# Attention with beacon keys followed by a two-layer MoE block: head pairs scored in two PSUM banks, values as the moving operand, 512-token chunks, and other loads for Q and K

## The chip, the cores and the metric

The kernel runs on one core of a Trainium2 chip. Five engines work side by side on their own instruction queues: TensorE (PE in the profile, its weight loads as PEld), VectorE (DVE), ScalarE (ACT), GpSimd (POOL) and SyncE (SP). Data comes from device memory by DMA transfers, which here are issued from the queues of POOL and SP. Matrix products go into PSUM, which has eight banks of 512 four-byte columns per partition. What counts is the device time of one execution in microseconds, as the median of several runs.

## What is computed

The inputs are fp32: q, k, v of 8 batches, 8 heads, 576 positions and 64 features; 16 beacon keys and values per head that every query sees; and two weight matrices.

```python
k_all = concatenate([beacon_k, k], axis=2)          # 592 keys
v_all = concatenate([beacon_v, v], axis=2)
scores = matmul(q, k_all.T) / 8
scores = where(causal, -1e9, scores)                # beacons are never masked
a = exp(scores - scores.max(-1)); a /= a.sum(-1) + 1e-9
x = matmul(a, v_all)                                # (8, 8, 576, 64)
x = x.transpose(0, 2, 1, 3).reshape(4608, 512)      # tokens x (heads, features)
h = x @ w_in                                        # 512 -> 2048
out = maximum(0.01 * h, h) @ w_out                  # 2048 -> 512
```

## The kernel before

A scheduler of the framework puts the instructions of each engine in an order that follows the written program with some reordering by readiness. Each engine then runs its own queue strictly in that order, and waits on semaphores where it needs another engine's result or a free buffer.

**Loads.** For each batch q, k and v are fetched by POOL's DMA queue in blocks of 128 positions, which also turns fp32 into bf16 on the way (`load_q`, `load_k`, `load_v`, L121 to L160); the beacons are the first 16 rows of the key blocks. The value tile `v_aug` holds 64 value columns and 64 columns of ones per head. The weights come in 16 loads from the same queue, spread over the first twelve steps.

**Heads.** The program runs 64 steps, one head each. In every second step `stage_transpose` (L162) turns two heads of q and k so that features lie on partitions: two heads fill 128 partitions, and DVE copies them out of PSUM. `stage_scores` (L185) takes one head, 64 partitions: for each block of 128 keys one matmul gives transposed scores (keys on partitions, queries along columns), only for the queries that see the block, and ACT takes the exponential of each block into `aT` (L202), six instructions a head. DVE zeroes the masked triangles by a multiplication (L209, L217). There is no maximum subtraction.

**Values.** `stage_av` (L225) makes the value block the stationary operand and `aT` the moving one, in two halves of 288 queries. The result has the 64 value features on partitions 0 to 63 and, from the ones, 64 copies of the row sum on partitions 64 to 127. The reciprocal is taken on ACT as exp(-ln(sum)):

```python
nc.scalar.activation(out=lnd[0:64, 0:qw], in_=av[64:128, 0:qw], func=AF.Ln)
nc.scalar.activation(out=recip[0:64, 0:qw], in_=lnd[0:64, 0:qw], func=AF.Exp, scale=-1.0)
```

and DVE multiplies by it on the way into `xT` (L249), which already has features on partitions, as the MoE part needs it.

**MoE.** For each batch of 576 tokens `moe1_fchunk` (L256) computes one of 16 blocks of 128 hidden features, in a piece of 512 tokens and one of 64, and ACT applies the leaky ReLU as Prelu (L271). `moe2_tchunk` (L278) accumulates 16 matmuls for 128 tokens and DVE copies the result out (L290); the 64 left-over tokens of two batches share one tile (`moe2_tailpair`, L293). The tables `MOE1_SCHED`, `MOE2A_SCHED` and `MOE2B_SCHED` place this work beside the heads of the next batches, and the last batch's part follows alone.

**PSUM.** Two banks' worth for transposes, four for scores and MoE together (`ps_acc`), two for the values.

Of the kernel before, what the change touches and what calls it, by code (L numbers as in the profile page):

```python
# [15 lines left out]
def kernel(  # L16
# [15 lines left out]
    L = S + NB  # L32
# [3 lines left out]
    assert DM == H * D  # L36

    KBLK = []
    l0 = 0
    while l0 < L:  # L40
        rows = min(128, L - l0)
        off = max(0, l0 - NB)
        KBLK.append((l0, rows, off, S - off))
        l0 += 128
    NKB = len(KBLK)

    QBLK = []
    s0 = 0
    while s0 < S:
        rows = min(128, S - s0)  # L50
        QBLK.append((s0, rows))
        s0 += 128
    NQB = len(QBLK)

    NJ = DM // 128
    NF = DF // 128
    TOKCH = [(0, 512), (512, S - 512)]
    OTCH = [(i * 128, min(128, S - i * 128)) for i in range((S + 127) // 128)]

    QCH = [(0, 288), (288, 288)]  # L60

    singles = ctx.enter_context(tc.tile_pool(name="singles", bufs=1))
    inpool = ctx.enter_context(tc.tile_pool(name="inpool", bufs=2))
    headpool = ctx.enter_context(tc.tile_pool(name="headpool", bufs=2))
    xpool = ctx.enter_context(tc.tile_pool(name="xpool", bufs=2))
# [3 lines left out]
    ps_tr = ctx.enter_context(tc.tile_pool(name="ps_tr", bufs=2, space=bass.MemoryType.PSUM))  # L69
    ps_acc = ctx.enter_context(tc.tile_pool(name="ps_acc", bufs=4, space=bass.MemoryType.PSUM))  # L70
    ps_av = ctx.enter_context(tc.tile_pool(name="ps_av", bufs=2, space=bass.MemoryType.PSUM))

    ident = singles.tile([128, 128], BF16, name="ident")
    with tc.high_priority():
        make_identity(nc, ident)

    mask_reg = singles.tile([128, 128], BF16, name="mask_reg")
    with tc.high_priority():
        nc.vector.memset(mask_reg, 1.0)
        nc.gpsimd.affine_select(  # L80
            out=mask_reg,
            in_=mask_reg,
            compare_op=ALU.is_ge,
            fill=0.0,
            base=0,
            channel_multiplier=-1,
            pattern=[[1, 128]],
        )

    w_in_sb = singles.tile([128, NJ, DF], BF16, name="w_in_sb")  # L90
# [5 lines left out]
    def _w_in_load(j, half):  # L96
        f0 = half * (DF // 2)
        return lambda: nc.gpsimd.dma_start(
            out=w_in_sb[:, j, f0 : f0 + DF // 2],
            in_=w_in_r[:, j, f0 : f0 + DF // 2],  # L100
        )

    def _w_out_load(c):
        return lambda: nc.gpsimd.dma_start(
            out=w_out_sb[:, c : c + 2, :], in_=w_out_r[:, c : c + 2, :]
        )

    weight_loads = []
    for half in range(2):
        for j in range(NJ):  # L110
            weight_loads.append(_w_in_load(j, half))
    for c in range(0, NF, 2):
        weight_loads.append(_w_out_load(c))

    def alloc_batch():
        q_nat = inpool.tile([128, NQB, H, D], BF16, name="q_nat")
        k_nat = inpool.tile([128, NKB, H, D], BF16, name="k_nat")
        v_aug = inpool.tile([128, NKB, H, D + 64], BF16, name="v_aug")
        return dict(q_nat=q_nat, k_nat=k_nat, v_aug=v_aug)

    def load_q(b, bt):  # L121
        q_nat = bt["q_nat"]
        for ci, (s0, rows) in enumerate(QBLK):
            nc.gpsimd.dma_start(  # L124
                out=q_nat[0:rows, ci, :, :],
                in_=q[b, :, s0 : s0 + rows, :].rearrange("h p d -> p h d"),
            )

    def load_k(b, bt):
        k_nat = bt["k_nat"]  # L130
        nc.gpsimd.dma_start(
            out=k_nat[0:NB, 0, :, :],
# [309 lines left out]
```

## Time and profile before

| | |
|---|---|
| median of 3 runs | 616.53 us (lowest 613.58) |
| span of the profiled execution, first to last instruction | 610.7 us |
| time of the profiled execution itself | not recorded apart from its span |
| matmul and weight-load instructions on PE | 2766 and 2816 recorded |
| ACT table loads at L243 and L246 | 80 and 79 |
| read from and written to device memory | 37.22 MB, 9.44 MB |

A row of the groups names the source line, the engine, the operation, the tiles written and read, the shapes and a count; behind the bar stand the busy time in us, the mean duration of one in ns, and the time the engine sat idle just ahead of these instructions with what ended it. A row of the timeline has the start and the duration in us, the engine, the line, and a count of merged instructions, with the idle time ahead of it in brackets. A row of the windows has the stretch and its length, the busy time of PE, PEld, DVE, ACT and POOL with counts, the granted clock of PE as a share of full speed, the DMA share and GB/s. Matmuls overlap in the record: the distance from start to start tells their pace, the duration does not.

### The profile page before, as it was taken

How to read it: one execution, taken by the hardware profiler on the slowest of the kernel's cores; microseconds unless marked ns; L12 is line 12 of the kernel's file. 1: busy time of each engine (PE TensorE's matmuls, PEld its weight loads, DVE VectorE, ACT ScalarE, POOL GpSimd, SP SyncE). 2: the span in 40 equal slices, each digit the busy share in tenths (PEclk: the TensorE clock that was granted, in tenths of full speed). 3: DMA queues.
4: the chain of work that ended last, by engine and by line, in shares of the span. 5: the costliest groups of instructions: out<-in, count | busy, mean ns of one | idle time of the engine just before them, and what ended most of it. 6: DMA issues, size and time to landing. Idle time of an engine off the chain costs nothing.

```text
span 610.7 us, 7832 instructions
## 1 busy us (share of the span) xinstructions
PE 470.3 (77%) x2766; PEld 226.2 (37%) x2816; DVE 174.1 (29%) x557; ACT 512.6 (84%) x1057; POOL 120.4 (20%) x159
## 2 busy tenths in 40 slices
PE   2867677876798697886888777886858876885696
PEld 1323333433344343443444333443424433442342
DVE  4233321342124412234223521234122421132101
ACT  0899989998999969999999979999799978997640
POOL 9885323020230303103230302303000000000000
PEclk9999888996889988997989978899789988897799
DMA  9999638024660706606561526616000100000002
GB/s 93 152 176 170 41 25 55 35 48 27 40 41 34 75 18 41 57 35 58 38 42 36 64 29 39 41 53 57 1 1 18 52 4 15 0 35 18 19 18 69
DMA packets 123432, 28.57 MB, mean 47 GB/s; under 512 B 115712, under 2 KB 117760, under 8 KB 123392
## 3 DMA queue, kind: packets, MB, share of 16 engines
q0 software_dynamic: 118144, 18.62, 41.3%
q1 hardware_dynamic: 5248, 9.44, 4.5%
q8 instruction: 22, 0.36, 0.3%
q14 instruction: 18, 0.15, 0.1%
HBM read 37.22 MB, written 9.44 MB: 76 GB/s over the span
## 4 chain that ended last, share of the span: by engine, by line
ACT 51%; PE 24%; issue 16%; DVE 6%; POOL 1%; DMA 1%; DVEq 0%; POOLq 0%
ACT L243 14%; PE acc L260 11%; ACT aT L202 11%; ACT L246 9%; ACT recip L246 6%; ACT lnd L243 6%; PE acc L195 5%; ACT gT L271 4%; PE acc L282 4%; DVE osb L290 3%; DVE xT L249 3%; PE acc L296 2%; PE av_ps L233 1%; ACT gtail L271 1%; DMA k_nat<-in_k_dram 1%
## 5 line engine op out<-in xcount | busy, mean ns | idle before, releaser
L260 PE MATMUL acc<-xT,w_in_sb 128*128 128x512 bf16 (+1 forms) x996 | 169.9, 329 | 33.0 <-ACT gT L271 25.2
L202 ACT ACTIVATE aT<-acc 128x512 bf16<-128x512 f32 (+5 forms) x384 | 123.6, 408 | 38.7 <-PE acc L195 37.5
L233 PE MATMUL av_ps<-aT,v_aug 128*128 128x288 bf16 (+4 forms) x512 | 85.3, 273 | 59.1 <-DVE xT L249 59.1
L260 PEld LDWEIGHTS <-w_in_sb 128*128 128x128 bf16 x1024 | 82.7, 111 | 118.9 <-issue 77.8
L249 DVE TENSOR_TENSOR xT<-av_ps,recip 64x288 bf16<-64x288 f32 x128 | 53.5, 447 | 253.9 <-ACT recip L246 253.8
L282 PE MATMUL acc<-w_out_sb,gT 128*128 128x512 bf16 x491 | 114.4, 382 | 0.8
L195 PE MATMUL acc<-qT_sb,kT_sb 64*128 64x512 bf16 (+5 forms) x384 | 82.6, 310 | 30.1 <-ACT gT L271 13.9
L243 ACT ACT_TABLE_LOAD x80 | 102.6, 1283 | 1.4
L246 ACT ACT_TABLE_LOAD x79 | 101.4, 1283 | 1.4
L271 ACT ACTIVATE gT<-acc 128x512 bf16<-128x512 f32 x128 | 76.6, 599 | 28.9 <-PE acc L260 26.6
L233 PEld LDWEIGHTS <-v_aug 128*128 128x128 bf16 (+1 forms) x512 | 41.0, 101 | 107.4 <-issue 80.6
L282 PEld LDWEIGHTS <-gT 128*128 128x128 bf16 x512 | 48.8, 98 | 54.7 <-issue 1.6
L124 POOL DMA_DIRECT2D q_nat<-in_q_dram x40 | 33.9, 878 | 98.1 <-PE tp_ps L168 95.1
L246 ACT ACTIVATE recip<-lnd 64x288 f32<-64x288 f32 x128 | 51.4, 436 | 0.9
L217 DVE TENSOR_TENSOR aT<-aT,mask_reg 128x128 bf16<-128x128 bf16 (+1 forms) x256 | 45.9, 212 | 18.8 <-ACT aT L202 16.4
L195 PEld LDWEIGHTS <-kT_sb 64*128 64x128 bf16 (+1 forms) x384 | 28.7, 102 | 59.8 <-issue 48.6
L243 ACT ACTIVATE lnd<-av_ps 64x288 f32<-64x288 f32 x128 | 46.9, 403 | 4.2 <-PE av_ps L233 3.3
L209 DVE TENSOR_TENSOR aT<-aT,mask_reg 128x112 bf16<-128x112 bf16 x64 | 13.5, 211 | 81.3 <-ACT aT L202 80.3
L148 POOL DMA_DIRECT2D v_aug<-in_beacon_v_dram x8 | 4.4, 548 | 156.2 <-PE av_ps L233 156.0
L140 POOL DMA_DIRECT2D k_nat<-in_k_dram x40 | 33.6, 861 | 1.4 <-DMA w_in_sb<-in_moe_w_in_dram 0.7
L157 POOL DMA_DIRECT2D v_aug<-in_v_dram x40 | 33.7, 868 | 0.0
L290 DVE COPY osb<-acc 128x512 f32<-128x512 f32 x32 | 21.9, 684 | 33.4 <-PE acc L282 33.0
(23 smaller groups left out, 185.0 us busy)
## 6 DMA issues: line engine op xcount, KB each, us to landing
out_dram<-osb SPq DMA_DIRECT2D x32, 256.0 KB, 2.0
q_nat<-in_q_dram POOLq DMA_DIRECT2D x32, 128.0 KB, 4.1
k_nat<-in_k_dram POOLq DMA_DIRECT2D x24, 128.0 KB, 4.1
v_aug<-in_v_dram POOLq DMA_DIRECT2D x24, 128.0 KB, 4.2
w_in_sb<-in_moe_w_in_dram POOLq DMA_DIRECT2D x8, 256.0 KB, 7.0
w_out_sb<-in_moe_w_out_dram POOLq DMA_DIRECT2D x8, 256.0 KB, 9.0
out_dram<-osb SPq DMA_DIRECT2D x8, 128.0 KB, 2.3
k_nat<-in_k_dram POOLq DMA_DIRECT2D x8, 112.0 KB, 3.2
```

The source lines that it names most:

```text
L124: nc.gpsimd.dma_start(out=q_nat[0:rows, ci, :, :], in_=q[b, :, s0 : s0 + rows, :].rearrange("h p d -> p h d"),)
L195: nc.tensor.matmul(out=acc[0:rows, 0:cw], lhsT=kT_sb[p0 : p0 + 64, l0_ : l0_ + rows], rhs=qT_sb[p0 : p0 + 64, c0 : c0 + cw], start=True, s ...
L202: nc.scalar.activation(out=aT[0:rows, ci, c0 - off : c0 - off + cw], in_=acc[0:rows, 0:cw], func=AF.Exp, scale=0.125,)
L217: nc.vector.tensor_tensor(out=aT[0:rows, ci, 0:rows], in0=aT[0:rows, ci, 0:rows], in1=mask_reg[0:rows, 0:rows], op=ALU.mult,)
L233: nc.tensor.matmul(out=av[0:128, lo - qs : qw], lhsT=v_aug[0:rows, ci, h, :], rhs=aT[0:rows, ci, lo - off : qs + qw - off], start=(bi == 0 ...
L243: nc.scalar.activation(out=lnd[0:64, 0:qw], in_=av[64:128, 0:qw], func=AF.Ln)
L246: nc.scalar.activation(out=recip[0:64, 0:qw], in_=lnd[0:64, 0:qw], func=AF.Exp, scale=-1.0)
L249: nc.vector.tensor_tensor(out=xT[(h % 2) * 64 : (h % 2) * 64 + 64, h // 2, qs : qs + qw], in0=av[0:D, 0:qw], in1=recip[0:64, 0:qw], op=ALU ...
L260: nc.tensor.matmul(out=acc[:, 0:tw], lhsT=w_in_sb[:, j, fc * 128 : (fc + 1) * 128], rhs=xT[:, j, ts : ts + tw], start=(j == 0), stop=(j == ...
L271: nc.scalar.activation(out=dst, in_=acc[:, 0:tw], func=AF.Prelu, alpha=0.01,)
L282: nc.tensor.matmul(out=acc[0:tw, :], lhsT=gT[:, fc, t0 : t0 + tw], rhs=w_out_sb[:, fc, :], start=(fc == 0), stop=(fc == NF - 1),)
L290: nc.vector.tensor_copy(out=osb[0:tw, :], in_=acc[0:tw, :])
```

## The change

Nearly all of the kernel is written anew; the mathematics is the same.

- **Loads of q and k.** They come as fp32 by SP's DMA queue, in pieces of two heads with 96 partitions and six successive positions (1536 bytes) each; POOL casts them to bf16 (for the first batch DVE casts q). Beacon keys are loaded apart, turned once per batch on PE, and copied by POOL into the first 16 columns of each `kT`. Position p x 6 + i lies on partition p, so the copies out of PSUM write with a step of six.
- **Weights** come in eight loads of twice the size, all issued in the first three steps.
- **Scores** are made for two heads at once, one on partitions 0 to 63 and one on 64 to 127, into the two banks of one PSUM tile, and one exponential covers both banks: five exponentials per pair of heads. The last 128 queries of key block 0 are packed beside block 2, and block 4 is padded to 128 queries.
- **Values.** `aT` is now the stationary operand and the value block with a single column of ones the moving one, 65 columns wide; 30 matmuls a pair. The sum lies in column 64 of each query's row; DVE takes the reciprocal and multiplies, and PE turns the result into `xT` by five transposes.
- **MoE** runs over nine chunks of 512 tokens across batch borders, all tiles full, in 40 steps of 16 + 16 matmuls. `xT` holds all tokens.
- **ACT tables.** One load of a set is placed at the start.
- **PSUM.** Four banks for scores (two tiles of two banks), two for transposes and values together (`mb`), two for the MoE.

The core of the new code (line numbers of the new kernel are L195 for `scores`, L246 for `values`, L288 for `moe1`):

```diff
+    nc.scalar.preload_act_table_set("natural_log_exp_and_others")
+    def load_qk(b, half, split):
...
+            raw = rawpool.tile([RP, 4, RI, D], FP32, name=name)
+            for e in range(2):
+                hs = slice(h0 + 2 * e, h0 + 2 * e + 2)
+                nc.sync.dma_start(
+                    out=raw[:, 2 * e : 2 * e + 2],
+                    in_=src[b, hs].rearrange("h (p i) d -> p h i d", i=RI),
+                )
+            for e in range(2):
+                eng = (nc.vector if n == 0 else nc.gpsimd) if split else nc.gpsimd
+                eng.tensor_copy(
+                    out=dst[:, :, h0 + 2 * e : h0 + 2 * e + 2, :],
+                    in_=raw[:, 2 * e : 2 * e + 2].rearrange("p h i d -> p i h d"),
+                )
+    def transposes(g):
...
+        for par in range(2):
+            ps_ = slice(par * 64, par * 64 + 64)
+            nc.gpsimd.tensor_copy(out=kT[ps_, 0:NB], in_=bkT[ps_, b, 2 * hp + par, :])
+        for src, dst in ((q_nat, qT), (k_nat, kT[:, NB : NB + S])):
+            ps = ps_mb.tile([128, 1024], BF16, name="mb", tag="mb")
+            for i in range(RI):
+                nc.tensor.transpose(
+                    ps[:, i * RP : (i + 1) * RP],
+                    src[:, i, hs, :].rearrange("p h d -> p (h d)"),
+                    ident[0:RP, 0:RP],
+                )
+            nc.vector.tensor_copy(
+                out=dst.rearrange("c (p i) -> c i p", i=RI),
+                in_=ps[:, 0:S].rearrange("c (i p) -> c i p", i=RI),
+            )
+    def scores(g):
...
+        for parts in SCORES:
+            sc = ps_sc.tile([128, 2, 512], FP32, name="sc", tag="sc")
+            c0 = parts[0][3]
+            for c, q0, w, col in parts:
+                for par in range(2):
+                    ps_ = slice(par * 64, par * 64 + 64)
+                    nc.tensor.matmul(
+                        out=sc[0 : ROWS[c], par, col - c0 : col - c0 + w],
+                        lhsT=kT[ps_, c * 128 : c * 128 + ROWS[c]],
+                        rhs=qT[ps_, q0 : q0 + w],
...
+            nc.scalar.activation(
+                out=aT[:, :, c0 : c0 + w], in_=sc[:, :, 0:w], func=AF.Exp, scale=0.125
+            )
...
+    def values(g):
...
+                    for c in range(t + 1):
+                        a0 = acol(c, q0)
+                        nc.tensor.matmul(
+                            out=avv[:, n, 0 : D + 1],
+                            lhsT=aT[0 : ROWS[c], par, a0 : a0 + 128],
+                            rhs=va[0 : ROWS[c], c, 2 * hp + par, :],
...
+            nc.vector.reciprocal(out=rec[:, n0:n1], in_=avv[:, :, D])
+            nc.vector.tensor_tensor(
+                out=x_nat[:, t0:t1].rearrange("p t e d -> p (t e) d"),
+                in0=avv[:, :, 0:D],
+                in1=rec[:, n0:n1, None].to_broadcast([128, n1 - n0, D]),
+                op=ALU.mult,
+            )
...
+    for g in range(NG + 2):
...
+            transposes(g)
+        if 1 <= g <= NG:
+            scores(g - 1)
+        if g >= 2:
+            values(g - 2)
+        if g >= NPAIR + 2:
+            moe_step(g - NPAIR - 2)
+    for m in range(NG - NPAIR, NPAIR * (NCH + 1)):
+        moe_step(m)
```

A step g thus makes the transposes of pair g, the scores of pair g - 1, the values of pair g - 2, and from g = 6 on one of the 40 MoE steps.

Three places show how the change moves instructions. ACT first, before: what follows the scores of one head (lnd and recip are the logarithm and the reciprocal of the row sums, aT the exponentials).

```order
L243 ACT_TABLE_LOAD
L243 ACTIVATE lnd<-av_ps 64x288 x2
L246 ACT_TABLE_LOAD
L246 ACTIVATE recip<-lnd 64x288 x2
L202 ACTIVATE aT<-acc 128x512
L202 ACTIVATE aT<-acc 128x64
L202 ACTIVATE aT<-acc 128x464
L202 ACTIVATE aT<-acc 128x336
L202 ACTIVATE aT<-acc 128x208
L202 ACTIVATE aT<-acc 80x80
```

ACT after, from its first instruction on (sc is the PSUM tile of two banks):

```order
L77 ACT_TABLE_LOAD
L215 ACTIVATE aT<-sc 128x2x512
L215 ACTIVATE aT<-sc 128x2x464 x2
L215 ACTIVATE aT<-sc 128x2x208
L219 ACTIVATE aT<-sc 80x2x128
```

Ten instructions a head, two of them loads, have become five for two heads; behind each pair's five stand four Prelus from the seventh pair on, and no further load.

POOL near the start, before: its queue behind the first k loads.

```order
L148 DMA v_aug<-in_beacon_v_dram 16x8x64
L157 DMA v_aug<-in_v_dram 112x8x64
L157 DMA v_aug<-in_v_dram 128x8x64 x3
L157 DMA v_aug<-in_v_dram 80x8x64
L98 DMA w_in_sb<-in_moe_w_in_dram 128x1024 x3
L124 DMA q_nat<-in_q_dram 128x8x64 x4
```

POOL after, at the same place (k_raw and q_raw are the fp32 tiles, the L178 copies write the beacon columns of kT):

```order
L160 DMA v_aug_95<-in_v_dram 128x8x64 x3
L164 DMA v_aug_95<-in_v_dram 80x8x64
L108 DMA w_in_sb<-in_moe_w_in_dram 128x4x512 x2
L137 CAST q_nat<-q_raw 96x6x128 x2
L137 CAST k_nat<-k_raw 96x6x128 x2
L108 DMA w_in_sb<-in_moe_w_in_dram 128x4x512 x2
L178 COPY kT<-bkT 64x16 x2
L146 DMA bk<-in_beacon_k_dram 128x64 x2
```

Before, POOL only issued transfers here; now casts of the next batch and the copies that the scores of pair 0 wait for stand in the same queue, behind value and weight loads.

PE in the middle of the program, before: between two groups of score matmuls (L195) stand value matmuls with 176 and 48 moving columns.

```order
L195 MATMUL acc<-qT_sb,kT_sb 128x64
L233 LDWEIGHTS v_aug
L233 MATMUL av_ps<-aT,v_aug 128x176
L233 LDWEIGHTS v_aug
L233 MATMUL av_ps<-aT,v_aug 128x48
```

PE after, in the middle, from the second block of scores (L204) to the values (L261):

```order
L204 MATMUL sc<-qT,kT 128x464
L293 LDWEIGHTS w_in_sb
L293 MATMUL acc<-xT,w_in_sb 128x512
L261 LDWEIGHTS aT
L261 MATMUL mb<-v_aug_96,aT 128x65
```

The values are loaded as weights no more: `aT` is, and each load is followed by 65 moving columns; a MoE matmul stands between the scores and the values.

More of the change, by code (lines that the diff above doesn't have):

```diff
@@ L31 @@
     NB = beacon_k.shape[2]
-    L = S + NB
     DM = moe_w_in.shape[0]
@@ L112 @@
[L112 to L123, printed above, removed]
+    xT = singles.tile([128, NJ, NTOK], BF16, name="xT")
```

459 lines of the change are left out of this document (178 added, 281 removed).

## The prediction

> **What bounds the kernel now.** I read the page's busy shares first, then its clock row, the chain of work that ended last, the groups kept apart by shape, and the timeline at four places.
>
> ```profile
> span 610.7 us, 7832 instructions
> PE 470.3 (77%) x2766; PEld 226.2 (37%) x2816; DVE 174.1 (29%) x557; ACT 512.6 (84%) x1057; POOL 120.4 (20%) x159
> ACT 51%; PE 24%; issue 16%; DVE 6%; POOL 1%; DMA 1%; DVEq 0%; POOLq 0%
> L243 ACT ACT_TABLE_LOAD x80 | 102.6, 1283 | 1.4
> L246 ACT ACT_TABLE_LOAD x79 | 101.4, 1283 | 1.4
> L249 DVE TENSOR_TENSOR xT<-av_ps,recip 64x288 bf16<-64x288 f32 x128 | 53.5, 447 | 253.9 <-ACT recip L246 253.8
> ```
>
> ACT is busy 84% of the span and holds half of the chain. Of its 512.6 us, 102.6 + 101.4 = 204 us are table loads: each head switches to the logarithm and back. The last row shows who suffers: DVE, and behind it PE, wait 253.8 us for that reciprocal. PE's 77% is not a full PE, as matmuls overlap in the record, so its true pace must come from distances between starts:
>
> ```profile
> 572.68 15.70 PE L260 MATMUL acc<-xT,w_in_sb 128*128 128x512 bf16 x110 [0.15 <-ACT gT L271]
> 588.22 13.98 PE L282 MATMUL acc<-w_out_sb,gT 128*128 128x512 bf16 x63
> 602.03 3.62 PE L296 MATMUL acc<-w_out_sb,gtail 128*128 128x512 bf16 x15
> 580.47 0.60 ACT L271 ACTIVATE gT<-acc 128x512 bf16<-128x512 f32 x1 [0.27 <-PE acc L260]
> 581.45 0.60 ACT L271 ACTIVATE gT<-acc 128x512 bf16<-128x512 f32 x1 [0.27 <-PE acc L260]
> 477.93 0.20 PE L168 MATMUL tp_ps<-ident,q_nat 64*128 64x64 bf16 x1
> 478.06 0.44 PE L174 MATMUL tp_ps<-ident,k_nat 128*128 128x128 bf16 x5
> 478.43 0.61 PE L195 MATMUL acc<-qT_sb,kT_sb 64*128 64x512 bf16 x3
> ```
>
> The four L282 tiles of 16 matmuls run from 588.22 to 602.03 (one record is missing): 13.81 / 64 = 0.216 us for 512 columns with a weight load each. In L260 one feature block (four matmuls of 512 columns, four of 64) repeats every 581.45 - 580.47 = 0.98 us, so a 64-column matmul with its load takes (0.98 - 4 x 0.216) / 4 = 29 ns. Linear in between: 128 columns 56 ns, 96 columns 42 ns. The 64-row transpose at 477.93 is followed only 130 ns later, where its 64 columns account for 29: changing between 64-row and 128-row operands costs about 0.1 us. The five k transposes confirm both (4 x 56 + 37 + 100 = 361 ns against 478.43 - 478.06 = 370).
>
> **The change, ACT.** These rows give an exponential's cost by length:
>
> ```profile
> L202 ACT ACTIVATE aT<-acc 128x512 bf16<-128x512 f32 x64 | 38.5, 602 | 24.9 <-PE acc L195 24.1
> L202 ACT ACTIVATE aT<-acc 128x208 bf16<-128x208 f32 x64 | 22.7, 354 | 1.7 <-PE acc L195 1.2
> L202 ACT ACTIVATE aT<-acc 128x64 bf16<-128x64 f32 x64 | 14.6, 228 | 0.0
> ```
>
> The slope is (602 - 228) / 448 = 0.835 ns a column. A pair of heads now has five instructions of 2 x 512, 2 x 464 twice, 2 x 208 and 2 x 128 columns: 1.03 + 2 x 0.95 + 0.53 + 0.38 = 3.84 us, for 32 pairs 123 us. 144 Prelus of 512 columns (0.60 each in the L271 rows above) are 86 us. All table loads but one, all logarithms and all reciprocals leave ACT: 123 + 86 + 1 = 210 us. ACT stops being the bound.
>
> **DVE and POOL.** DVE takes over the reciprocal and the scaling.
>
> ```profile
> L217 DVE TENSOR_TENSOR aT<-aT,mask_reg 128x128 bf16<-128x128 bf16 x192 | 39.0, 219 | 18.8 <-ACT aT L202 16.4
> L209 DVE TENSOR_TENSOR aT<-aT,mask_reg 128x112 bf16<-128x112 bf16 x64 | 13.5, 211 | 81.3 <-ACT aT L202 80.3
> L290 DVE COPY osb<-acc 128x512 f32<-128x512 f32 x32 | 21.9, 684 | 33.4 <-PE acc L282 33.0
> L181 DVE COPY qT_sb<-tp_ps 128x576 bf16<-128x576 bf16 x32 | 14.6, 456 | 16.2 <-PE acc L195 10.7 <-PE tp_ps L168 5.4
> ```
>
> Masks: 8 ns for 16 columns, 0.5 ns a column, so 224, 768 and 256 columns take 0.27 + 0.54 + 0.28 = 1.09 us. The q and k copies now write every sixth element: between 0.46 (L181) and 0.75 (L290's 684 ns carried on to 576 columns at about 1 ns each); I take 0.75, the row without packing. Scaling (384 and 256 columns out of PSUM) 0.55 + 0.42 by the same slope, two short reciprocals 0.2 each by the shortest mask row, the xT copy 0.46. Together 4.4 us a pair and 0.68 us per output tile: 5.1 us of each step below, hidden behind PE, which needs twice that. If the masks fell to 1 ns a column a step would have 5.7 us: still hidden.
>
> POOL gets eight casts of 768 columns per batch, which no row shows. Its memset and affine-select bound them:
>
> ```profile
> 0.81 0.20 POOL masks.py:197 MEMSET ident<- 128x128 bf16 x1 [0.29 <-POOLq L426]
> 2.69 0.31 POOL masks.py:199 TENSOR_SCALAR_AFFINE_SELECT ident<-ident 128x128 bf16<-128x128 bf16 x1
> L157 POOL DMA_DIRECT2D v_aug<-in_v_dram x40 | 33.7, 868 | 0.0
> L148 POOL DMA_DIRECT2D v_aug<-in_beacon_v_dram x8 | 4.4, 548 | 156.2 <-PE av_ps L233 156.0
> L104 POOL DMA_DIRECT2D w_out_sb<-in_moe_w_out_dram x8 | 5.7, 715 | 1.7 <-DMA w_out_sb<-in_moe_w_out_dram 1.2 <-DMA w_in_sb<-in_moe_w_in_dram 0.4 <-issue 0.2
> w_out_sb<-in_moe_w_out_dram POOLq DMA_DIRECT2D x8, 256.0 KB, 9.0
> ```
>
> With about 0.1 us fixed, 128 columns cost 0.1 to 0.2 us, so a cast takes 0.7 to 1.35 us; I take 1.0, the middle, as neither row is a copy. Eight casts, five value loads, three beacon loads and eight tiny copies are 8 + 4.3 + 1.6 + 1.2 = 15 us a batch against 40 us of PE: hidden, in the steady part.
>
> **The start, S.** There POOL is not hidden. By the order in the section on the change, the beacon columns of kT, without which no score of a pair starts, stand on POOL behind everything queued earlier. Up to the copies of pair 5 that is 20 casts (20 us), 6 + 2 beacon loads (4.4), 10 value loads (8.7), 8 weight loads of about 0.7 (5.6), a dozen copies (about 2) and 3 us of setup: 44 us. Three waits come on top: about 3 us for the first k, and some 6 us for weight loads whose slot is still in flight (such loads took 9.0 us to land). So pair 5 is released near 53 us, and the MoE matmuls, which stand behind its scores on PE, flow from about 57 us. The ends are 48 (short casts, no slot waits) and 72 (long casts, and 8 us more of waits). The q and k loads on SP are hidden in this: they are asked for ahead of POOL's queue and in longer pieces.
>
> **PE, the new bound.** MoE: 9 chunks x 16 x 4 + 36 x 16 = 1152 matmuls of 512 columns x 0.216 = 249 us. For each pair PE also does 12 transposes of 96 columns (0.51), five of the normalized output (0.27), 30 value matmuls of 65 columns at 29 ns (0.87), and 12 score matmuls (one head's columns: 216 + 196 + 142 + 89 + 56 + 56 = 0.755 us). Three blocks of scores mean six changes of operand height: 0.6.
>
> The scores of the two heads use rows 0 to 63 and 64 to 127 of the array. No two such matmuls follow each other in this trace. Ends: one after another, 1.51 us, as one head's do; or overlapped, 0.755. The nearest row, 477.93, shows a cost and no overlap when the height changes, so it does not decide; I keep both ends. Then PE waits for ACT: the last score block needs the bank pair that the second exponential frees, 0.42 (matmul to ACT) + 1.03 + 0.95 = 2.4 us after the first block at least, of which other work fills some 1.75 to 2.2; wait 0.65 (overlapped) or 0.4. A pair costs 0.51 + 0.27 + 0.87 + 0.6 + 1.51 + 0.4 = 4.2 us one after another, 3.65 overlapped; I take the middle, 3.9. Of 32 pairs about 27 lie behind the 57 us.
>
> [...]
>
> The clock decides whether these rates hold.
>
> ```profile
> 18.55 0.61 PE L195 MATMUL acc<-qT_sb,kT_sb 64*128 64x512 bf16 x1
> 195.92 0.39 PE L195 MATMUL acc<-qT_sb,kT_sb 64*128 64x512 bf16 x1
> core 0: 610.7 us, clock 0.905
> 283.00:289.60 6.60, 3.96 (x17) 1.76 (x17) 0.51 (x2) 6.48 (x11) 0.00 (x0) 0.50 0.36 24
> 313.60:351.00 37.40, 30.66 (x196) 15.48 (x198) 14.94 (x45) 34.71 (x72) 6.67 (x9) 1.00 0.47 54
> ```
>
> The same matmul takes 0.61 us at 18.55 and 0.39 later: the start runs at half clock (the clock column has no record there). At 283 the grant falls to 0.50 where PE is 60% busy (3.96 of 6.60), and it holds 1.00 where PE is 82% busy (30.66 of 37.40). A step of the changed kernel has 32 dense MoE matmuls (6.9 us) in about 10.8, with attention work in most of the rest, so I take the full clock after the start.
>
> **Sum.** 57 + 249 + 27 x 3.9 = 105 + the last copy and store (0.7 + 2.0, as below) = 414 us of span.
>
> ```profile
> 605.69 0.69 DVE L304 COPY osb<-acc 128x512 f32<-128x512 f32 x1 [2.76 <-PE acc L296]
> out_dram<-osb SPq DMA_DIRECT2D x32, 256.0 KB, 2.0
> ```
>
> The median before, 616.5, is 5.8 above the profiled span, 610.7; no other time of the profiled execution is recorded. With the same surplus: 419.5 us.
>
> **Rivals.**
> 1. Small matmuls do not stay at 29 ns. That rate is seen four at a time; now 18 or 30 stand in a row, each with a load. If loads no longer hide, the spacing is the load's own duration, 101 ns below: 30 x 0.072 x 27 = 58 us more, 478. Against it: five transposes in a row kept 56 ns.
>
> ```profile
> L233 PEld LDWEIGHTS <-v_aug 128*128 128x128 bf16 x448 | 35.8, 101 | 104.7 <-issue 79.8 <-DVE xT L249 8.9 <-DVE aT L209 5.9
> ```
>
> [...]
> 2. The clock is granted as before, 0.905 on average, as each attention stretch drops it. The 354 us of PE work become 354 / 0.905 = 391: 457 us.
> 3. Slower than before: the half clock stays. 354 us of PE work become 708, the total 774; it decides once over 56% of that work runs at 0.50 (420 + 354 x 0.56 = 617). For it: the first 60 us do run so. Against: the MoE stretches at 1.00.
> 4. A lighter case: overlapped scores, short casts and waits that other work fills: 48 + 249 + 27 x 3.2 + 9 = 392.
>
> That the loads stay is no rival: in the built order ACT has a single load.
>
> **Chances.** Forecast 0.70 (its own range, from its ends of S and of a pair: 398 to 450), small matmuls 0.09, clock 0.11, slower 0.03, lighter 0.06, and 0.01 for a gain that other waits eat up within 2% (about what a measurement of this kernel tells from no change). The range 394 to 462 holds the forecast, the clock case and about half of the lighter one: over 0.8. All but the last two kinds are faster: 0.96.
>
> **What would show it.** Right: ACT near 210 us busy and one table load; L293 and L305 0.216 us apart; L261 starts 29 ns apart; a step of 10 to 11.5 us; MoE dense from about 57 us; clock 1.00 after the start. The two heads' scores starting together, or 0.2 us apart, decide between the ends. Wrong: PE waiting on POOL kT copies after 60 us, on DVE's x_nat, or a clock row with fives in the middle.

## The result, and the profile after

The changed kernel took 524.58 us (median of 4 runs, 523.9 to 525.74) beside 616.19 us for the kernel before on the same chip: a ratio of 0.853, 95% interval 0.8483 to 0.8577. One of the four runs of the kernel before, of 1085.5 us, is not in the ratio, which goes by fast runs alone. The changed kernel is faster, as forecast, but by 92 us and not by 197, and its time lies outside the range of 394 to 462.

From the page of the changed kernel: the span, the busy shares, the granted clock in 40 slices of 13 us, the chain (the work that ended last, followed back from the end to what released it), and four groups (columns as before: busy us, mean ns | idle ahead of them and its releaser).

```profile
span 522.0 us, 7381 instructions
PE 407.5 (78%) x3048; PEld 208.6 (40%) x3048; DVE 239.3 (46%) x369; ACT 201.0 (39%) x305; POOL 115.7 (22%) x205
PEclk9999999987888887998888998888799889999999
PE acc L293 26%; PE acc L305 24%; DVE kT L187 12%; DVE qT L187 9%; PE mb L261 7%; DMA bk<-in_beacon_k_dram 4%; PE sc L204 3%; PE mb L279 3%; DVE osb L313 2%; DMA v_aug<-in_v_dram 2%; DMA k_raw<-in_k_dram 1%; PE mb L182 1%; ACT aT L215 1%; SPq L131 1%; DVE aT L232 0%
...
L261 PE MATMUL mb<-v_aug,aT 128*128 128x65 bf16 (+1 forms) x960 | 56.7, 217 | 64.6 <-DVE qT L187 35.3
...
L187 DVE COPY qT<-mb 128x576 bf16<-128x576 bf16 x32 | 66.4, 2075 | 9.6 <-PE mb L182 7.2
L187 DVE COPY kT<-mb 128x576 bf16<-128x576 bf16 x32 | 70.4, 2199 | 0.0
L137 POOL CAST q_nat<-q_raw 96x768 bf16<-96x768 f32 x28 | 22.7, 828 | 39.5 <-issue 38.8
```

ACT has done what was forecast: 201 us, and 1% of the chain. What was not forecast: 21% of the chain lies on the two DVE copies of L187, which take 2.1 to 2.2 us each, and the clock row has sevens and eights where it was to be full. One step of the middle in PE's timeline of the changed kernel:

```profile
306.40 0.42 PE L182 MATMUL mb<-ident,q_nat 96*128 96x96 bf16 x6
306.66 0.42 PE L182 MATMUL mb<-ident,k_nat 96*128 96x96 bf16 x6
307.01 0.59 PE L204 MATMUL sc<-qT,kT 64*128 64x512 bf16 x4
307.53 0.39 PE L293 MATMUL acc<-xT,w_in_sb 128*128 128x512 bf16 x1
309.34 0.53 PE L261 MATMUL mb<-v_aug,aT 128*128 128x65 bf16 x12 [1.43 <-DVE qT L187]
309.71 0.38 PE L293 MATMUL acc<-xT,w_in_sb 128*128 128x512 bf16 x1
310.02 0.37 PE L204 MATMUL sc<-qT,kT 64*128 64x336 bf16 x4
311.29 0.42 PE L261 MATMUL mb<-v_aug,aT 128*128 128x65 bf16 x5 [0.89 <-DVE kT L187]
...
320.47 0.42 PE L182 MATMUL mb<-ident,q_nat 96*128 96x96 bf16 x6
```

and DVE's timeline of the same step:

```profile
307.21 2.08 DVE L187 COPY qT<-mb 128x576 bf16<-128x576 bf16 x1
309.00 2.23 DVE L187 COPY kT<-mb 128x576 bf16<-128x576 bf16 x1
```

The q and k transposes fill both PSUM tiles of `mb`. The first value group needs the one that q's copy frees, the second the one that k's copy frees. PE stands 1.43 us for the first and 0.89 us for the second, and the step takes 14.1 us where 10 to 11.5 were expected. Over the whole span these two waits come to 57.2 us, by the table of waits (who waits for whom; us in total, times, longest):

```profile
PE mb L261 <- DVE qT L187: 35.3, 29, 1.5
PE mb L261 <- DVE kT L187: 21.9, 24, 1.1
```

A second cost follows, in the windows of the same kernel (the stretch and its length, busy us of PE, PEld, DVE, ACT and POOL, then the granted clock):

```profile
307.90:311.30 3.40, 1.08 (x19) 0.65 (x18) 3.40 (x4) 2.27 (x3) 2.96 (x4) 1.00 0.21 77
311.30:314.70 3.40, 3.40 (x31) 2.24 (x31) 2.38 (x7) 1.43 (x4) 2.40 (x5) 0.50 0.00 0
128.30:416.20 287.90, 241.14 (x1917) 125.27 (x1916) 152.48 (x234) 125.54 (x190) 55.76 (x102) 0.89 0.30 53
```

Through 3.4 us with the two waits PE works 1.08 us; through the next 3.4 us it gets half the clock, although it is then busy throughout. In these steps the trace has the half clock only in stretches of 3.4 or 6.8 us. Over the 21 steps from pair 10 to pair 31 the clock averages 0.89, and a step takes 13.7 us.

The start is late too. One piece of the chain in order of time (start, length):

```profile
25.27 18.98 DMA bk<-in_beacon_k_dram
```

PE's timeline at its end, then POOL's with the value loads of batch 1:

```profile
44.38 0.26 PE L148 MATMUL mb<-ident,bk 128*128 128x128 bf16 x1 [17.51 <-DMA bk<-in_beacon_k_dram]
```

```profile
37.75 0.84 POOL L156 DMA_DIRECT2D v_aug<-in_v_dram  x1 [4.13 <-DMA w_in_sb<-in_moe_w_in_dram]
41.58 0.89 POOL L160 DMA_DIRECT2D v_aug<-in_v_dram  x1 [2.99 <-DMA w_in_sb<-in_moe_w_in_dram]
```

The Prelus of the MoE in the view by source line (shortest, median and longest in ns, first and last start in us):

```profile
L300 ACT ACTIVATE gT<-acc x144: 597/597/599, 89.7 to 500.8; 128x512 bf16<-128x512 f32 x144
```

PE is idle from 26.9 to 44.4 us for the beacon keys of batch 1, which were asked for behind value and weight loads; the value loads behind them wait for weights to land. The first Prelu runs at 89.7 us, where the MoE was to flow from 57.

### The profile page after: what moved, and what is told of

It is laid out like the page before. It is cut to its first block, busy times and chain, and to the rows that moved or that the text cites. A ratio compares the mean times of both kernels' runs of the same rounds, so it can differ in the third digit from the quotient of the medians.

```text
span 522.0 us, 7381 instructions
## 1 busy us (share of the span) xinstructions
PE 407.5 (78%) x3048; PEld 208.6 (40%) x3048; DVE 239.3 (46%) x369; ACT 201.0 (39%) x305; POOL 115.7 (22%) x205
## 4 chain that ended last, share of the span: by engine, by line
PE 63%; DVE 24%; DMA 7%; issue 3%; ACT 1%; SPq 1%; POOL 0%; DVEq 0%; POOLq 0%
PE acc L293 26%; PE acc L305 24%; DVE kT L187 12%; DVE qT L187 9%; PE mb L261 7%; DMA bk<-in_beacon_k_dram 4%; PE sc L204 3%; PE mb L279 3%; DVE osb L313 2%; DMA v_aug<-in_v_dram 2%; DMA k_raw<-in_k_dram 1%; PE mb L182 1%; ACT aT L215 1%; SPq L131 1%; DVE aT L232 0%
## 5 line engine op out<-in xcount | busy, mean ns | idle before, releaser
L215 ACT ACTIVATE aT<-sc 128x928 bf16<-128x928 f32 (+2 forms) x128 | 105.3, 856 | 187.1 <-PE sc L204 186.8
L293 PE MATMUL acc<-xT,w_in_sb 128*128 128x512 bf16 x576 | 165.9, 423 | 0.0
L305 PE MATMUL acc<-w_out_sb,gT 128*128 128x512 bf16 x576 | 129.5, 379 | 0.0
L261 PE MATMUL mb<-v_aug,aT 128*128 128x65 bf16 (+1 forms) x960 | 56.7, 217 | 64.6 <-DVE qT L187 35.3
L305 PEld LDWEIGHTS <-gT 128*128 128x128 bf16 x576 | 56.4, 98 | 67.9
L261 PEld LDWEIGHTS <-aT 128*128 128x128 bf16 (+1 forms) x960 | 48.2, 112 | 82.9 <-issue 79.1
L187 DVE COPY qT<-mb 128x576 bf16<-128x576 bf16 x32 | 66.4, 2075 | 9.6 <-PE mb L182 7.2
L187 DVE COPY kT<-mb 128x576 bf16<-128x576 bf16 x32 | 70.4, 2199 | 0.0
L178 POOL COPY kT<-bkT 64x16 bf16<-64x16 bf16 x64 | 12.7, 199 | 198.1 <-PE sc L204 100.8
L204 PE MATMUL sc<-qT,kT 64*128 64x128 bf16 (+5 forms) x384 | 50.0, 335 | 8.2 <-POOL kT L178 6.7
L271 DVE TENSOR_TENSOR x_nat<-mb,rec 128x384 bf16<-128x384 f32 x64 | 31.3, 490 | 2.0
L137 POOL CAST k_nat<-k_raw 96x768 bf16<-96x768 f32 x32 | 27.7, 889 | 5.9 <-DMA k_raw<-in_k_dram 5.9
L279 PE MATMUL mb<-ident,x_nat 128*128 128x128 bf16 (+1 forms) x160 | 24.9, 272 | 0.7 <-DVE x_nat L271 0.7
L204 PEld LDWEIGHTS <-kT 64*128 64x128 bf16 (+1 forms) x384 | 14.0, 105 | 28.3 <-issue 15.7
L279 PEld LDWEIGHTS <-x_nat 128*128 128x128 bf16 (+1 forms) x160 | 15.3, 126 | 18.9 <-DVE x_nat L271 10.5
L270 DVE RECIPROCAL rec<-mb 128x6 f32<-128x6 f32 x64 | 12.2, 190 | 23.3 <-PE mb L261 23.3
## 6 DMA issues: line engine op xcount, KB each, us to landing
w_in_sb<-in_moe_w_in_dram POOLq DMA_DIRECT2D x4, 512.0 KB, 19.6
w_out_sb<-in_moe_w_out_dram POOLq DMA_DIRECT2D x4, 512.0 KB, 13.8
```

Source lines behind the costliest of these rows:

```text
L137: eng.tensor_copy(out=dst[:, :, h0 + 2 * e : h0 + 2 * e + 2, :], in_=raw[:, 2 * e : 2 * e + 2].rearrange("p h i d -> p i h d"),)
L187: nc.vector.tensor_copy(out=dst.rearrange("c (p i) -> c i p", i=RI), in_=ps[:, 0:S].rearrange("c (i p) -> c i p", i=RI),)
L204: nc.tensor.matmul(out=sc[0 : ROWS[c], par, col - c0 : col - c0 + w], lhsT=kT[ps_, c * 128 : c * 128 + ROWS[c]], rhs=qT[ps_, q0 : q0 + w], ...
L215: nc.scalar.activation(out=aT[:, :, c0 : c0 + w], in_=sc[:, :, 0:w], func=AF.Exp, scale=0.125)
L261: nc.tensor.matmul(out=avv[:, n, 0 : D + 1], lhsT=aT[0 : ROWS[c], par, a0 : a0 + 128], rhs=va[0 : ROWS[c], c, 2 * hp + par, :], start=(c = ...
L271: nc.vector.tensor_tensor(out=x_nat[:, t0:t1].rearrange("p t e d -> p (t e) d"), in0=avv[:, :, 0:D], in1=rec[:, n0:n1, None].to_broadcast( ...
```

## The experiments

Every kernel here starts from the changed one; times are medians of 4 runs (the last one of 7), ratios are to the kernel before, which ran beside each of them on the same chip. The runs used four chips, so where small differences count the ratios are compared. Theory A: the strided copies hold the PSUM tiles that the values wait for. Against it stood that the exponentials or the clock would set the step anyway, and for the start, that POOL's own queue and not the order of the loads was late.

### Reading with the step instead of writing with it

```diff
             nc.vector.tensor_copy(
-                out=dst.rearrange("c (p i) -> c i p", i=RI),
-                in_=ps[:, 0:S].rearrange("c (i p) -> c i p", i=RI),
+                out=dst.rearrange("c (p i) -> c p i", i=RI),
+                in_=ps[:, 0:S].rearrange("c (i p) -> c p i", i=RI),
             )
```

> The two copies behind the six q or k transposes (L187) write the rows in order and read the PSUM with a step of six; all else stays. In the changed kernel each takes 2.1 to 2.2 us, and the value matmuls of the next part wait for the PSUM buffers that they hold (35.3 and 21.9 us over the span). Theory A, the strided write of 2-byte elements is what is slow and its wait sets the step: the copy falls to about 0.8 us, the waits of L261 on the copies go below 15 us together, a step falls from 13.8 to about 11 us, the time to 440 to 460. Rival B, a step of six costs the same on the side of the reads: copies stay near 2.1 and the time within 1% of 524.6. Rival C, copies fall but PE waits for the exps or for the clock in their place: copies near 0.8, time above 500.

(The read takes six values 96 columns apart, then begins one column further on; the expectation calls it a step of six.) Measured: 424.51 us, ratio 0.692 (0.6872 to 0.6969). From its page, the span, the clock row and the two copies:

```profile
span 426.7 us, 7332 instructions
PEclk9999999999999999999999999999999999999999
L187 DVE COPY qT<-mb 128x576 bf16<-128x576 bf16 x32 | 24.0, 751 | 8.2 <-PE mb L182 6.2
L187 DVE COPY kT<-mb 128x576 bf16<-128x576 bf16 x32 | 24.0, 749 | 0.4 <-PE sc L204 0.3
```

and its Prelus by source line:

```profile
L300 ACT ACTIVATE gT<-acc x144: 596/597/598, 79.6 to 405.6; 128x512 bf16<-128x512 f32 x144
```

The order on PE, ACT and POOL is that of the changed kernel, only two access patterns differ, and 95 us of span are gone: more than expected. (The profiled execution is the longest of the four; between the medians lie 100 us.) The copies take 0.75 us, PE's waits on them fall from 57.2 to 0.8 us, and the clock is full. Rivals B and C fall.

The q transposes of pairs 10 to 31 give the step (by source line, 132 of them, first and last start), in the changed kernel:

```profile
L182 PE MATMUL mb<-ident,q_nat x132: 203/206/208, 128.3 to 416.4; 96*128 96x96 bf16 x132
```

and in this one:

```profile
L182 PE MATMUL mb<-ident,q_nat x132: 203/206/208, 104.0 to 324.4; 96*128 96x96 bf16 x132
```

(416.4 - 128.3) - (324.4 - 104.0) = 67.7 us over 21 steps: 3.22 us a step. Of the other 27.6 us, 10.1 lie ahead of the first Prelu (89.7 against 79.6), about 14 between it and pair 10, and 3 in the end.

### No reorder at all

```diff
-            nc.vector.tensor_copy(
-                out=dst.rearrange("c (p i) -> c i p", i=RI),
-                in_=ps[:, 0:S].rearrange("c (i p) -> c i p", i=RI),
-            )
+            nc.vector.tensor_copy(out=dst, in_=ps[:, 0:S])
```

> The same two copies without any reorder: contiguous on both sides. The positions of q and k stay in the order of the transposes, so the scores are those of permuted positions: this leaves out the reorder and its output is not the reference's; every instruction and size is otherwise kept. Theory A: the copy takes 0.46 to 0.75 us, the step about 10.8 us, the time 435 to 455, the clock row without the sevens and eights of the middle. Rival C, the clock or the exps set the step anyway: copies short, waits of L261 move to exps (L215) or PE stays at the half clock, time above 500. Were e1 still slow and this fast, the stride and not its side is the cost.

Measured: 426.1 us, ratio 0.694 (0.6906 to 0.6973), copies of 448 ns. 0.3 us less per copy buys nothing. The scheduler ordered PE differently here, so the two steps (10.6 us here, 10.5 in the run before) are not a comparison of the copy alone; that PE waits only 0.8 us in all for copies of 0.75 us is what says that they are hidden.

### One strided copy at a time

The branch keeps the strided write for q alone, or (with the condition reversed) for k alone. PE's order is again unchanged.

```diff
+            if dst is qT:
+                nc.vector.tensor_copy(
+                    out=dst.rearrange("c (p i) -> c i p", i=RI),
...
+            else:
+                nc.vector.tensor_copy(
+                    out=dst.rearrange("c (p i) -> c p i", i=RI),
...
```

> Only the copy of q keeps the strided write (2.1 us); that of k reads with the step (0.75 us). The order on TensorE is that of the changed kernel. There the step of 13.9 us holds a wait of 1.43 us on q's copy, one of 0.89 us on k's, and about 3.4 us at half clock. Theory F, waits and clock are two costs, and the clock falls only where the waits of a step together are long enough: the wait on q stays at 1.4, that on k goes, no sevens and eights in the clock row, a step of about 11.9 us, the time 455 to 470. Rival G, any wait of over a microsecond brings the half clock: a step of 13 to 13.6 us, clock 0.93 or less in the middle, the time 490 to 510.

> The reverse: q's copy reads with the step (0.75 us), k's keeps the strided write (2.2 us). k's copy would end 3.7 us after the first transpose of the step, and the second group of value products is due 2.6 us after it: a wait of about 1 us on k's copy, none on q's. Theory F: no half clock in the middle, a step of about 11.5 us, the time 445 to 460. Rival G: half clock also here, a step of 12.5 to 13.2 us, 475 to 500. Were the time below 432, the copy of k alone is hidden and q's is the whole cause.

Measured: 461.85 us, ratio 0.7519 (0.7461 to 0.7578), with q's strided; 454.63 us, 0.7382 (0.7336 to 0.7428), with k's. With q's copy strided, the table of waits, the first value group of one step in PE's timeline, and the window of the 21 steps from pair 10 to pair 31:

```profile
PE mb L267 <- DVE qT L188: 38.1, 30, 1.6
```

```profile
276.17 0.53 PE L267 MATMUL mb<-v_aug,aT 128*128 128x65 bf16 x12 [1.42 <-DVE qT L188]
```

```profile
111.30:354.50 243.20, 215.71 (x1917) 109.51 (x1916) 124.51 (x234) 123.63 (x190) 57.58 (x104) 1.00 0.37 64
```

The table of waits and the window with k's copy strided:

```profile
PE mb L267 <- DVE kT L188: 21.1, 24, 1.6
```

```profile
110.20:347.90 237.70, 217.24 (x1917) 111.79 (x1916) 124.97 (x234) 123.27 (x190) 58.20 (x104) 1.00 0.38 66
```

Theory F holds in both: one wait a step, and full clock (1.00) in these steps. (Ahead of them, from 57 to 81 us, the run with q's copy strided has the half clock: 0.97 on average over the first 60 us, 0.74 from 60 to 100.) A step takes 243.2 / 21 = 11.58 us with q's and 237.7 / 21 = 11.32 with k's; the run without strided writes needs 220.2 / 21 = 10.49 (220.4 less the 0.2 within the last group). One strided copy makes a step 1.09 us (q's) or 0.83 us (k's) longer, together 1.92; both make it 3.22 us longer. Longer waits are not the reason: 38.1 and 21.1 us apart are 59.2, beside 57.2 with both. The other 1.30 us come only with both, and with them comes the half clock: at its average of 0.89, (1 - 0.89) x 287.9 / 21 = 1.5 us a step, an estimate.

### The copies left slow, but covered

```diff
-        if g >= 2:
-            values(g - 2)
         if g >= NPAIR + 2:
             moe_step(g - NPAIR - 2)
+        if g >= 2:
+            values(g - 2)
```

> The changed kernel with its slow copies (2.1 to 2.2 us, step-six writes), but in each step the MoE part stands ahead of the values, so seven to eight products of 0.216 us and the scores lie between the transposes and the first value product that takes their PSUM buffer. Theory A, the copies cost only through the two buffers that the values wait for: the waits of L261 on the copies fall from 57 to under 15 us although each copy is as long as before, the step comes to about 10.7 us, the time to 430 to 450 (the steps before MoE flows stay long). Rival D, the long copies cost in another way (VectorE's own time, its share of the PSUM or the clock): time above 490.

Measured: 456.69 us, ratio 0.7452 (0.7389 to 0.7515): the mechanism as expected, the size above the range. Its copies by source line:

```profile
L187 DVE COPY qT<-mb x32: 2067/2078/2187, 17.0 to 352.9; 128x576 bf16<-128x576 bf16 x32
```

and its waits (us, times, longest):

```profile
PE mb L261 <- DVE kT L187: 10.3, 9, 1.4
...
PE mb L261 <- DVE qT L187: 3.3, 7, 1.5
```

The copies are as slow as ever, yet the waits on them fall from 57.2 to 13.6 us, the granted clock is 0.999, and 68 us are gone. What a slow copy cost here depended on what stood between the transposes and the next user of their PSUM. The span is still 28.4 us longer than with the short copies: 16.0 us of that lie ahead of pair 10, as the first Prelu still comes only at 89.3 us, and 12.2 us in the 21 steps behind it, which take 10.7 to 11.5 us, 11.07 on average, where 10.49 was reached.

### Each short copy done twice

```diff
+            for _ in range(2):
+                nc.vector.tensor_copy(
+                    out=dst.rearrange("c (p i) -> c p i", i=RI),
+                    in_=ps[:, 0:S].rearrange("c (i p) -> c p i", i=RI),
+                )
```

> The copies that read with a step, each done twice: 1.5 us of VectorE for q and 1.5 for k with no strided write in it. Theory A, the length of the copy is what counts, beyond a cover of scores on PE of some 1.5 us behind the transposes: a step of 11.5 to 12.5 us where 0.75 gave 10.47 and 2.1 to 2.2 gave 13.9; the time 455 to 485. Rival E, the strided write itself disturbs (its writes delay others, or it takes the SBUF from ScalarE and TensorE): with no strided write the time stays below 435 although VectorE is busier by 48 us.

Measured: 429.01 us, ratio 0.6998 (0.6936 to 0.706); outside the 455 to 485 of theory A. That looks like rival E, but the scheduler had seen the second copies and had put MoE products ahead of the values, so that length was not all that changed. PE's timeline behind the transposes of a step:

```profile
250.56 1.04 PE L294 MATMUL acc<-xT,w_in_sb 128*128 128x512 bf16 x4
251.54 0.37 PE L205 MATMUL sc<-qT,kT 64*128 64x336 bf16 x4
251.85 0.39 PE L294 MATMUL acc<-xT,w_in_sb 128*128 128x512 bf16 x1
```

As a test of the length alone it decides nothing; that the step stayed at 10.49 us on average under 48 us more of VectorE work agrees with the run before: cover decides. For longer copies the scheduler thus rearranges; for the strided write it arranged PE exactly as for the read with a step, so it gave the strided copy no more cover.

### The start: beacon keys and weights

First with the slow copies: the beacon keys of batch 1 beside those of batch 0, and apart from that the weights one load a step.

```diff
     load_beacon_k(0)
+    load_beacon_k(1)
     load_qk(0, 1, True)
...
-                    load_beacon_k(b + 1)
+                    if b > 0:
+                        load_beacon_k(b + 1)
```

```diff
-    for f, i in weights[:2]:
-        f(i)
-    weights = weights[2:]
+    weights[0][0](0)
+    weights = weights[1:]
...
-            for f, i in weights[:2]:
-                f(i)
-            weights = weights[2:]
+            for f, i in weights[:1]:
+                f(i)
+            weights = weights[1:]
```

> The beacon keys of batch 1 are loaded beside those of batch 0, ahead of the values and the weights in POOL's queue; the copies stay as they are. In the changed kernel their transpose ends a wait of PE of 17.5 us at 44.4 us, behind a DMA that was issued behind value and weight loads. Theory, that wait is pure loss: it goes, MoE flows from about 75 us instead of 93, the time falls by 14 to 20 us, to 505 to 511. Rival, what is late next takes over (POOL's casts of batch 1's q and k, the value loads that wait for the weights' slots): a gain below 6 us, time 518 to 525.

> One load of 512 KB of the weights in each step instead of two, one ahead of the loop instead of two; the order of the rest stays. Theory, the weights' transfers in the way make the loads of the start late (batch 1's beacon keys were issued at 24.6 us and came 19 us later): the wait at 44.4 us shrinks to 5 to 10 us and the time falls by 6 to 12 us, to 512 to 519. Rival, POOL's own queue (descriptors and casts) is what is late: time within 1% of 524.6. Slower, if the last weights now come after the first MoE parts need them: a wait of L293 or L305 on DMA of w_in or w_out in the trace.

Measured: 510.77 us (ratio 0.8322, 0.8283 to 0.8362) and 516.81 us (0.8431, 0.8381 to 0.8481): 14 and 8 us less than the changed kernel, both within the times that their theories gave, the first at the slow end; the first Prelu comes at 77.9 and 81.4 us. But spreading the weights left a wait of 16.0 us on those keys (40.8 us instead of 44.4 at its end), so it gained in another way than expected.

Then on top of the read with a step: first the same edit of the beacon keys, and next that together with the weights one a step behind the transposes, none ahead of the loop:

```diff
-            for f, i in weights[:2]:
-                f(i)
-            weights = weights[2:]
             transposes(g)
+            for f, i in weights[:1]:
+                f(i)
+            weights = weights[1:]
```

> The copies read with the step (as the run that read the PSUM with a step) and the beacon keys of batch 1 come ahead of values and weights. With the slow copies the early beacon keys gave 14 us, and the wait that followed them (7.4 us of PE on POOL's small copies, behind value loads that wait for weights to land) stood where it was. Theory, the two causes lie in different stretches and add: 424.5 less 10 to 14, so 410 to 415. Rival, with short copies the start reaches the weights' wait sooner and that is late next: a gain below 6 us, 418 to 425.

> As the run before, and no weights ahead of the loop: one load of 512 KB after the transposes of each step, w_in in steps 0 to 3, w_out in 4 to 7 (first used in steps 6 and 10). Theory, what is late after the beacon keys is POOL's queue, whose loads wait for weights to land: PE's wait on POOL's kT copies falls below 2 us, MoE flows by about 50 us and the time is 398 to 408. Rival, the values of batch 1 or the casts of its q and k (0.85 us each) are late anyway: 408 to 415. Slower than the run before if a weight comes late: L293 or L305 waiting for a DMA.

Measured: 420.99 us (0.6865, 0.6794 to 0.6937) and 417.47 us (0.6812, 0.6752 to 0.6872): a miss twice. The first gained 3.5 us where 10 to 14 were expected, as its rival had it, and its interval overlaps that of the read with a step alone (0.6872 to 0.6969), so that even this gain is not clear of noise. PE then stood 14.0 us on POOL's copies into kT:

```profile
PE sc L204 <- POOL kT L178: 14.0, 2, 10.7
```

The second lies outside both of its ranges. That wait is gone, but PE stood 10.5 us at 59 us for the beacon keys of batch 2, again asked for behind a weight load:

```profile
59.44 0.26 PE L148 MATMUL mb<-ident,bk 128*128 128x128 bf16 x1 [10.47 <-DMA bk<-in_beacon_k_dram]
```

### All of it

Loading and turning the beacon keys become two functions; they are loaded a batch ahead and turned at the fourth pair.

```diff
+    load_beacon_k(1)
+    turn_beacon_k(0)
...
                 elif hp == 1:
-                    load_beacon_k(b + 1)
                     load_qk(b + 1, 1, False)
...
+                elif hp == 3:
+                    turn_beacon_k(b + 1)
+                    if b + 2 < B:
+                        load_beacon_k(b + 2)
```

> The run that read with a step, had batch 1's beacon keys first and the weights one per step, and now also every later batch's beacon keys loaded a batch ahead, their transpose put at the fourth pair of the batch before. In that run (417.5) PE waited 10.5 us at 59 us for the beacon keys of batch 2, issued behind a weight load. Theory, that wait is loss: the time falls to 405 to 411. Rival, the transfers themselves bound the start (210 GB/s over the first 80 us, all queues busy) and the values or q and k of batch 1 and 2 are late next: 413 to 418.

Measured: 407.07 us, ratio 0.661 (0.6568 to 0.6653), as the theory had it: the lowest median of the study, 22% below the changed kernel (0.661 / 0.853). PE in 40 slices, from its page:

```profile
PE   0275899999999999999999999999999999999996
```

and the Prelus by source line:

```profile
L304 ACT ACTIVATE gT<-acc x144: 596/597/602, 57.3 to 383.7; 128x512 bf16<-128x512 f32 x144
```

Its span is 404.9 us at a granted clock of 0.998; PE is dense from the sixth slice on. One step further: the beacon keys ahead of the first casts, and the values of batch 0 ahead of the second half of q and k.

```diff
-    load_qk(0, 0, True)
     load_beacon_k(0)
     load_beacon_k(1)
+    load_qk(0, 0, True)
     turn_beacon_k(0)
-    load_qk(0, 1, True)
     load_v(0)
+    load_qk(0, 1, True)
```

> The version of 407.1 with the beacon keys of batches 0 and 1 ahead of everything in POOL's queue (there the first pair's transposes waited until 17.8 us for them, behind two casts) and the values of batch 0 ahead of the second half's q and k casts (the first values waited for them until 34.6 us). Theory, these waits of PE are loss: first MoE activation at about 52 instead of 57.3 us, the time 400 to 404. Rival, the start is held by the transfers (222 GB/s over its first 60 us), which this does not lessen: within 1% of 407.1.

Measured: 407.75 us, ratio 0.6667 (0.6638 to 0.6696): no gain. PE's waits in the version of 407.07 us:

```profile
PE mb L152 <- DMA bk<-in_beacon_k_dram: 17.8, 1, 17.8
PE mb L265 <- DMA v_aug<-in_v_dram: 3.5, 2, 2.6
PE sc L208 <- POOL kT L182: 2.2, 4, 1.0
```

and here:

```profile
PE mb L152 <- DMA bk<-in_beacon_k_dram: 9.6, 1, 9.6
PE sc L208 <- POOL kT L182: 8.0, 2, 5.0
PE mb L265 <- DMA v_aug<-in_v_dram: 6.0, 2, 3.4
```

The wait on the keys lost 8.2 us, those on POOL's copies and the values grew by 8.3. This fits the rival, a start held by its transfers; no run lessened the bytes, so it is not shown. The execution whose waits stand here had the half clock from 46.3 to 56.5 us (0.82 on average from 40 to 50 us, 0.67 from 50 to 60), so its later first Prelu (60.9 us) is not the doing of the order alone.

## Why the prediction was wrong, point by point

The span came out 108 us above the forecast's 414. The runs split that: the strided writes 95.3 us (522.0 to 426.7), the order of the start's loads 21.8 us (426.7 to 404.9), and 9.1 us the other way. (These are single profiled executions; by the medians the first two are 100.1 and 17.4 us.)

- **"The q and k copies now write every sixth element: between 0.46 (L181) and 0.75 ...; I take 0.75 ..."** This is the step that failed first. Both ends came from copies that write in order; the bound above was no bound for a strided write, which took 2.08 to 2.20 us. The 0.75 was exact for the other side: the copy that reads with a step takes 0.75.
- **"5.1 us of each step below, hidden behind PE, which needs twice that."** The second half of the same error. A share of the step hid nothing: these copies stand between two users of the same two PSUM tiles, with 0.9 us of PE's work as cover (307.01 to 307.91 above). At 0.75 us that was enough (0.8 us of waits in all), at 2.1 it was not (57.2); with the MoE part put in between, most of the wait was gone again (13.6 left).
- **"so I take the full clock after the start."** In the steps of the middle right for each run with one wait a step or none (1.00 in the windows of the runs with one strided copy and, from 100 to 360 us, of the run without), wrong for two (0.89). The clock's rival (457 us) gave an average of 0.905; the steps had 0.89, but as a result of waits that this rival did not have. The reading under it was of the wrong stretch: the 3.96 of 6.60 us at 283 is PE's share while the clock was already halved, and the 3.4 us ahead of it (279.5 to 282.9) have PE busy for 1.39 us. In the changed kernel too the half clock comes behind the idle stretch (1.08 of 3.40 us from 307.90, then 0.50). So in these traces the least busy 3.4 us of a step tells more of the clock than its average.
- **The start, S = 57.** The first Prelu came at 89.7 us, beyond the upper end of 72. Of the 32.7 us, 10.1 were the strided copies, which make the steps without MoE long as well, and 22.3 the loads (79.6 to 57.3 in the best version). The sum counted POOL's instructions, with 4.4 us for beacon loads as time to issue; that a load asked for behind 512 KB pieces took 19 us to land, and that PE's queue stood on it for 17.5, was not in it. The weight loads themselves, which the sum let land in the 9.0 us of loads half their size, took 19.6 (w_in) and 13.8 us (w_out) in the page's median. That the best version starts its Prelus at 57.3 us does not confirm S, as it has another order of loads. POOL's casts, feared at 0.7 to 1.35 us, took 0.83 to 0.89, inside that range.
- **A pair costs 3.9, the middle of 3.65 and 4.2.** A step of 10.49 less 32 x 0.216 leaves 3.58: just below the lower end. 27 x 0.32 = 8.6 us, which is most of the 9.1 the other way. The row at 307.01 above shows why: four score matmuls of 512 and 464 columns for two heads take 0.52 us to the next start, where one head alone would need 0.41 and two in a row 0.82, estimated from the 0.216 us of 512 columns. The two heads' products start 4 ns apart (307.010 and 307.014, 307.236 and 307.240).
- **Small matmuls at the pace of their loads.** This rival fell: twelve value matmuls from 309.34 to 309.71 are 31 ns apart.
- **ACT 210 us, one table load, MoE at 0.216.** As forecast: 201 us and one load; sixteen L305 products of the changed kernel, from 302.95 to the next row at 306.40, are 0.216 apart.
- **The sums.** The ends 398 and 450 do not follow from the stated ends of S and of a pair, which give 404 (48 + 249 + 27 x 3.65 + 8.5) and 443 us (72 + 249 + 27 x 4.2 + 8.5), with 8.5 for the last copy, the store and the surplus. The surplus of 5.8 us sets the median beside the span of another execution: each run of the changed kernel is only 1.9 to 2.0 us above its own span. Neither explains the miss.

The strided write took 2075 / 576 = 3.6 ns an element, against 751 / 576 = 1.3 when the step is on the read side. No run varied the length of the step, so why the write is the dear side was not shown.

## What to carry to other kernels

Bound a strided access by a strided row, on the side where it stands; without one, leave the upper end open. Before an operation is called hidden, name the buffer it holds and count what the waiting engine has to do until it needs it: the share of busy time says nothing about that. And a 16 KB load on which a queue stands goes ahead of the half-megabyte loads, for the next batch as for the first.

## What the runs showed of the hardware

- The same 128 x 576 copy of two-byte elements from PSUM took 0.45 us in order on both sides, 0.75 us reading with a step of 192 bytes, and 2.07 to 2.2 us writing with a step of 12 bytes.
- The clock fell to half (0.50) with no idle stretch longer than 1.43 us in the step: 3.4 us with only 1.08 us of work came ahead. One wait of 1.42 us a step did not bring it in the steps from pair 10 on (1.00). Where the border lies stays open: in the changed kernel, stretches of 3.4 us in which PE was 53 to 65% busy were followed by either clock (1.80 of 3.40 us from 284.0 us, then 1.00; 2.20 of 3.40 from 171.4, then 0.50).
- The waits add, their costs do not: 38.1 and 21.1 us of waits apart, 57.2 together, but 1.09 and 0.83 us a step apart and 3.22 together, as the half clock comes on top (0.89 on average, beside 1.00 with one strided copy).
- Two score products on rows 0 to 63 and 64 to 127 of the array ran at the same time: their starts are 4 ns apart, and four of them take 0.52 us to the next start.
